# Feature attention and experts on one core: where small ties and token sums run, and when the first chunk's operands and the first weights are made

## The chip, the cores and the metric

The kernel runs on one core of a Trainium2 chip. The metric is the device time of one execution in microseconds; the kernel before was timed three times. Each engine of the core (TensorE, VectorE, ScalarE, GpSimd, and SyncE, which issues all the DMAs here) works through a queue of its own in order, and waits for the others by semaphores.

## The reference

Two parts follow each other. The first is attention with random features, for 4 batches, 8 heads, 576 tokens and 64 values a head:

```python
def phi(x):                                   # x is q or k, scaled
    proj = np.einsum('bhsd,md->bhsm', x, omega)
    h = proj - np.sum(x * x, axis=-1, keepdims=True) / 2.0
    h = h - np.max(h, axis=-1, keepdims=True)
    return np.exp(h) / np.sqrt(m)
kv = np.einsum('bhsm,bhsd->bhmd', k_p, v)
num = np.einsum('bhsm,bhmd->bhsd', q_p, kv)
den = np.einsum('bhsm,bhm->bhs', q_p, z)[..., None] + 1e-06
```

Its output, 2304 tokens of 512 values, goes into a mixture of 8 experts: a gate (`x @ w_gate`, then 8 rounds of normalizing rows and columns), and for each expert `np.maximum(x @ w1[e], 0) @ w2[e]`, weighted by the gate and summed over the experts.

## The kernel before

**Attention stage.** The work is cut into 36 jobs: 18 for k, 18 for q. A job takes half the heads of 256 rows (or the remaining 64 rows of two batches, `kr` and `qr`) through steps: transposes on TensorE (L323), a copy of them, the products with omega (`pp`, L335), the maxima on VectorE (L338, into `sqs`), the offset `cn` (L340, from the maxima and the sums of squares), the exponentials (L348 to L351), then for k the products with v (L360), for q transposes (L415), the products with kv (L435), the division (L438 to L442) and transposes (L453) into the token layout `xf`. The list `jobs` gives the order: k first, then k and q in turn, at the end q alone. In each turn of the loop one job is started and every job under way goes one step (`tick`), so the jobs overlap. `ensure_loads` issues the loads of q, k and v some jobs ahead, and calls `squares` for the keys of the jobs to come (a key serves two jobs).

**Squares.** `squares` computes the sums of squares of a key: a Square on ScalarE into a scratch `sq` (two buffers), then a fold by halves on GpSimd (L302, L303) and a negation (L304). Ahead of the Square stands a *tie*: eight numbers of the newest `cn` are written into the scratch (L297, on GpSimd), so that the Square can't be placed before that job. Two other places have such ties: the first weights' load (L177) and the first split of w1 (L221).

**Token operands.** Three chunks of 768 tokens. When a chunk's tokens are there, `token_operands` makes seven operands of it, one a tick: sums or differences of quarters of `xf` in place (L110: on GpSimd for the first two chunks, on VectorE for the last), a rounded copy (`xs`, L125, ScalarE) and the difference from it (L126, VectorE). Each operand is written to DRAM (`xd`, L128) from one of four buffers; those of the last chunk are used at once (`first`), the others are read back later. `xf` has two buffers.

**Expert stage.** 16 units of half an expert; in each, seven first-layer products a chunk (`first`, L549) and seven second-layer products a token pair (`second`, L650), with weights that `stage` loads and `split` takes apart into a rounded part and the rest (L190 on GpSimd, L222 on ScalarE, L223). The first unit's w1 is loaded and split during the attention stage, at fixed places of the job list.

The order in which each engine gets its instructions isn't that of the program: it is fixed when the program is built, by a planner that puts an instruction in as soon as its operands are there by its own reckoning, earlier program text first. The ties are there to steer it.

Of the kernel before, what the change touches and what calls it, by code (L numbers as in the profile page):

```python
# [12 lines left out]
ALU = mybir.AluOpType  # L13
AX = mybir.AxisListType


def raw(ap):

    return ap.bitcast(F32)
# [3 lines left out]
def moe_attention_kernel(  # L23
# [23 lines left out]
    nc = tc.nc  # L47
# [43 lines left out]
    ORDER = [1, 5, 6, 3, 7, 2, 4]  # L91
# [4 lines left out]
    def token_tile():  # L96
        return xs.tile([P, 2, 2, HL], F32R, tag="xs", bufs=XSB, name="xs")

    def token_operands(c, x):

        def q(r, h):
            h = 1 - h
            return x[:, 2 * r : 2 * r + 2, h * HL : (h + 1) * HL]

        last = c == NCH - 1
        gate_steps = logits(c, x)
        next(gate_steps)

        def sub(o, a, b):
            (nc.vector if last else nc.gpsimd).tensor_tensor(o, a, b, op=ALU.subtract)  # L110

        for i in ORDER:
            if i == 5:
                sub(q(0, 0), q(0, 1), q(0, 0))
            elif i == 6:
                sub(q(0, 0), q(1, 1), q(0, 0))
            elif i == 7:
                sub(q(0, 1), q(1, 1), q(0, 1))  # L120
            elif i == 4:
                sub(q(0, 0), q(1, 0), q(0, 0))
            o = {3: q(1, 1), 7: q(0, 1), 2: q(1, 0)}.get(i, q(0, 0))
            t = token_tile()
            nc.scalar.copy(t[:, 0], o)  # L125
            nc.vector.tensor_tensor(t[:, 1], o, raw(t[:, 0]), op=ALU.subtract)  # L126
            xdram[c, i] = xd.tile([P, 2, 2, HL], F32, name=f"xd{c}_{i}")
            nc.sync.dma_start(out=xdram[c, i], in_=raw(t))  # L128
            if last:
                xop[0, c, i] = t  # L130
                first(0, c, i, 0)
                first(0, c, i, 1)
            next(gate_steps, None)
            yield


    def logits(c, x):


        nt = CT // 2  # L140
        lgs = []
        for h in range(2):
            lp = bank("lp")
            for k in range(KD):
                nc.tensor.matmul(
                    lp[k * GC : (k + 1) * GC, :HL], lhsT=wgs[:, k, :], rhs=x[:, k, h * HL : (h + 1) * HL],
                    start=True, stop=True,
                )
            lg = sc.tile([P, HL], F32, tag="lg", bufs=2, name="lg")
            nc.scalar.copy(lg, lp[:, :HL])  # L150
            lgs.append(lg)
        yield
        for h, lg in enumerate(lgs):
            gp = bank("gp")
            for j in range(nt):
                nc.tensor.transpose(gp[:, j * P : (j + 1) * P], lg[:, j * P : (j + 1) * P], ident)
            t0 = c * CT + h * nt
            nc.vector.tensor_reduce(
                prob[:, t0 : t0 + nt, :],
                gp[:, : nt * P].rearrange("p (t a e) -> p t e a", a=KD, e=GC)[:, :, :E, :],  # L160
                axis=AX.X, op=ALU.add,
            )
# [4 lines left out]
    tmp = {}  # L167

    last_cn = []

    def stage(u, w):
        e, fb = units[u]
        f0 = fb * FB * P
        for r in range(2):
            wst[u, w, r] = t = wp.tile([P, 2, 2, HD], F32, tag="st", bufs=4, name="st")
            if u == 0:
                nc.gpsimd.tensor_copy(t[:, 0, 0, :8], last_cn[-1])  # L177
            if w == 1:
                src = w1[e][r * HD : (r + 1) * HD, f0 : f0 + FB * P]
            else:  # L180
                src = w2[e][f0 + r * HD : f0 + (r + 1) * HD, :]
            nc.sync.dma_start(out=t.rearrange("p k h c -> p k (h c)"), in_=src.rearrange("(k p) c -> p k c", p=P))

    def split(u, w, i):

        def q(r, h):
            return wst[u, w, r][:, :, 1 - h if w == 1 else h]

        def tt(o, a, b, op=ALU.subtract):
            nc.gpsimd.tensor_tensor(o, a, b, op=op)  # L190


        if w == 1:

            if i == 5:
                tmp[u] = wp.tile([P, 2, HD], F32, tag="t", bufs=1, name="t")
                tt(tmp[u], q(0, 1), q(1, 1), ALU.add)
            elif i == 6:
                tt(tmp[u], tmp[u], q(0, 0))
            elif i == 3:  # L200
                tt(tmp[u], q(1, 0), tmp[u])
            elif i == 7:
                tt(q(0, 1), q(0, 0), q(0, 1))
            o = {1: q(0, 0), 7: q(0, 1), 2: q(1, 0), 4: q(1, 1)}[i] if i not in (5, 6, 3) else tmp[u]
        else:

            if i == 5:
                tt(q(0, 0), q(0, 1), q(0, 0))
            elif i == 6:
                tt(q(0, 0), q(0, 0), q(1, 1))  # L210
            elif i == 7:
                tt(q(0, 1), q(1, 1), q(0, 1))
            elif i == 4:
                tt(q(0, 0), q(1, 0), q(0, 0), ALU.add)
            o = {3: q(1, 1), 7: q(0, 1), 2: q(1, 0)}.get(i, q(0, 0))
        pool = wp if w == 1 else op_
        bufs = 7 * w
        hi = pool.tile([P, 2, HD], F32R, tag=f"w{w}h", bufs=bufs, name="wh")
        lo = pool.tile([P, 2, HD], F32R, tag=f"w{w}l", bufs=bufs, name="wl")
        if u == 0 and w == 1:  # L220
            nc.gpsimd.tensor_copy(hi[:, 0, :8], last_cn[-1])  # L221
        nc.scalar.copy(hi, o)  # L222
        (nc.vector if u > 0 or (w == 2 and i in (1, 6, 7, 4)) else nc.gpsimd).tensor_tensor(lo, o, raw(hi), op=ALU.subtract)  # L223
        wt[u, w, i] = (hi, lo)
# [20 lines left out]
    def prepare_gate():  # L245

        nc.gpsimd.memset(wgs, 0.0)
        nc.sync.dma_start(out=wgs[:, :, :E], in_=w_gate.rearrange("(k p) e -> p k e", p=P))
# [37 lines left out]
    sqt = {}  # L286
# [3 lines left out]
    def squares(which, key):  # L290

        t = rawt[which, key]
        n = 1 if key[0] == "r" else 2
        s = sc.tile([P, H, n, D], F32, tag="sq", bufs=2, name="sq")
        o = sc.tile([P, H, n, 3], F32, tag="sqs", bufs=10, name="sqs")
        if last_cn:
            nc.gpsimd.tensor_copy(s.rearrange("p h j d -> p (h j d)")[:, :8], last_cn[-1])  # L297
        nc.scalar.activation(s, t[:, :H], AF.Square, scale=1.0 / math.sqrt(2.0 * math.sqrt(D)))
        w = D
        while w > 2:  # L300
            w //= 2
            nc.gpsimd.tensor_tensor(s[..., :w], s[..., :w], s[..., w : 2 * w], op=ALU.add)  # L302
        nc.gpsimd.tensor_tensor(o[..., :1], s[..., :1], s[..., 1:2], op=ALU.add)  # L303
        nc.gpsimd.tensor_scalar_mul(o[..., 2], o[..., 0], -1.0)  # L304
        sqt[which, key] = o
# [103 lines left out]
    def q_job(key, hh, t0):  # L409
# [48 lines left out]
        if done_q[c] == CT:  # L458
            yield from token_operands(c, xf[c])
# [234 lines left out]
    jobs = []  # L694

    def k_of(b):
        return [("k", (b, i // 2), i % 2) for i in range(4)]

    def q_of(b):
        return [("q", (b, i // 2), i % 2, 4 * b + i // 2 * 2) for i in range(4)]  # L700

    def kr(p):
        return ("k", ("r", p), 0)

    def qr(p):
        return ("q", ("r", p), 0, 4 * B + p)

    def mix(a, b):
        o = []
        for i in range(max(len(a), len(b))):  # L710
            o += a[i : i + 1] + b[i : i + 1]
        return o

    jobs += k_of(0) + [kr(0)]
    jobs += mix(k_of(1), q_of(0))
    jobs += mix(k_of(2) + [kr(1)], q_of(1) + [qr(0)])
    jobs += mix(k_of(3), q_of(2))
    jobs += q_of(3) + [qr(1)]

    need, seen = [], set()  # L720
# [20 lines left out]
    def tick():  # L741
        for it in list(active):
            jb, gen = it
            try:
                next(gen)
            except StopIteration:
                active.remove(it)

    ensure_loads(0)
    for i, jb in enumerate(jobs):  # L750
        if i == 12:
            prepare_gate()
        if i == 16:
            stage(0, 1)
        if i >= 22 and i % 2 == 0 and (i - 22) // 2 < 7:
            split(0, 1, ORDER[(i - 22) // 2])
        if i == 30:
            stage(0, 2)
        gen = k_job(jb[1], jb[2]) if jb[0] == "k" else q_job(*jb[1:])
        active.append((jb, gen))  # L760
        tick()
        ensure_loads(i + 1)
# [19 lines left out]
    for j, i in enumerate(ORDER):  # L782
        split(0, 2, i)
        if j < AHEAD:
            first(*todo.pop(0))

    gate = sinkhorn()
    for s, (u, n) in enumerate(steps):
        c = n // (CT // 2)
# [11 lines left out]
        for k, i in enumerate(ORDER):  # L801
# [3 lines left out]
            if k < ((5, 5, 4) if s > 2 else (3, 4, 3))[n % 3] and todo:  # L805
                pc = todo.pop(0)
                first(*pc)
                j = ORDER.index(pc[2])
# [44 lines left out]
```

## Time and profile before

| | us |
|---|---|
| median of three runs (lowest, highest) | 1634.56 (1632.02, 1638.07) |
| the profiled execution | 1634.42 |
| its span, first to last instruction | 1632.6 |
| TensorE busy in the span | 1584.5 |
| VectorE busy | 1379.9 |
| ScalarE busy | 777.3 |
| GpSimd busy | 312.4 |

A span's busy time counts instructions that compute; what an engine waits or issues is not in it. The attention stage fills about the first 200 us of the span, the experts the rest. The engines are named PE (TensorE), PEld (its weight loads), DVE (VectorE), ACT (ScalarE), POOL (GpSimd) and SP (SyncE) in the profile; L126 is line 126 of the kernel before.

### The profile page before, as it was taken

Reading aid. Unit: us, or ns where it says so; the run is one execution under the profiler, and the core shown is the slowest. Engines: PE = TensorE matmul, PEld = TensorE weight load, DVE = VectorE, ACT = ScalarE, POOL = GpSimd, SP = SyncE. Lnnn points to the kernel's source line nnn. Section 1 sums busy time; section 2 is a strip of 40 time slices with the busy share of each in tenths; the row PEclk is TensorE's granted clock in tenths of the full one; section 3 lists DMA queues with packets and bytes.
Section 4 is the critical chain, followed back from the end, with each engine's and each line's share of the span. In section 5 each row is a group of like instructions: output and inputs, shape, how many; then the busy total and the mean of one; then the engine's idle time right before and its main releaser. Section 6 shows DMA issues by size and latency. Waiting matters only on the chain.

```text
span 1632.6 us, 31484 instructions
## 1 busy us (share of the span) xinstructions
PE 1584.5 (97%) x12318; PEld 1551.6 (95%) x12318; DVE 1379.9 (85%) x2714; ACT 777.3 (48%) x1396; POOL 312.4 (19%) x340
## 2 busy tenths in 40 slices
PE   7899799999999999999999999999999999999998
PEld 5778699999999999999999999999999999999997
DVE  3788888998888898989888888989898888889777
ACT  5788654544434444534444444434344444444333
POOL 5585230111111010201111111102011111110003
PEclk9999999999999999999999999999999999999999
DMA  9442866666656565666565665656666556655562
GB/s 237 122 157 73 329 246 216 216 208 218 201 195 213 186 221 198 222 204 232 204 219 197 203 217 179 229 193 229 203 220 218 205 197 206 213 178 192 181 226 77
DMA packets 105315, 329.80 MB, mean 202 GB/s; under 512 B 14800, under 2 KB 43984, under 8 KB 105168
## 3 DMA queue, kind: packets, MB, share of 16 engines
q1 hardware_dynamic: 105168, 327.79, 59.5%
q8 instruction: 98, 1.61, 0.4%
q14 instruction: 49, 0.40, 0.1%
HBM read 306.53 MB, written 21.23 MB: 201 GB/s over the span
## 4 chain that ended last, share of the span: by engine, by line
PE 86%; DVE 7%; ACT 2%; POOL 2%; DMA 2%; issue 1%; SPq 0%; DVEq 0%; ACTq 0%; POOLq 0%
PE hx L549 24%; PE x L650 23%; PE hz L549 18%; PE z L650 11%; PE w L650 6%; PE pp L335 2%; DVE out L676 1%; DVE sm L586 1%; POOL sq L302 1%; DVE bl L586 1%; DVE sqs L338 1%; PE kv L360 1%; DVE xs L126 1%; ACT ex L348 0%; DMA xs<-xd 0%
## 5 line engine op out<-in xcount | busy, mean ns | idle before, releaser
L549 PE MATMUL hx<-xs,wh 128*128 128x384 f32 x1536 | 374.3, 337 | 2.0 <-ACT xs L125 1.4
L676 DVE SCALAR_TENSOR_TENSOR out<-x,prob,out 128x256 f32<-128x256 f32 x497 | 233.3, 476 | 65.8 <-PE x L650 64.3
L549 PE MATMUL hz<-xs,wh 128*128 128x384 f32 x1152 | 281.5, 336 | 2.1 <-ACT xs L125 1.1
L549 PEld LDWEIGHTS hx<-xs,wh 128*128 128x128 f32 x1536 | 270.1, 189 | 3.5 <-issue 3.2
L190 POOL TENSOR_TENSOR st<-st 128x512 f32<-128x512 f32 x80 | 131.7, 1646 | 700.1 <-DVE wl L223 697.1
L549 PEld LDWEIGHTS hz<-xs,wh 128*128 128x128 f32 x1152 | 202.4, 188 | 2.9 <-issue 1.3
L549 PE MATMUL hx<-xs,wl 128*128 128x384 f32 x768 | 199.4, 337 | 0.0
L628 ACT ACTIVATE bh<-hr 128x512 fp32r<-128x512 f32 x144 | 91.2, 634 | 222.0 <-PE x L650 217.0
L676 DVE SCALAR_TENSOR_TENSOR out<-z,prob,out 128x256 f32<-128x256 f32 x252 | 120.0, 476 | 58.0 <-PE z L650 57.2
L222 ACT CAST wh<-st 128x512 fp32r<-128x512 f32 x176 | 105.1, 621 | 110.9 <-PE hx L549 44.8
L624 ACT CAST sh<-sm 128x512 fp32r<-128x512 f32 x144 | 89.7, 623 | 139.9 <-PE z L650 100.1
L549 PE MATMUL hz<-xs,wl 128*128 128x384 f32 x576 | 150.1, 335 | 0.0
L549 PEld LDWEIGHTS hx<-xs,wl 128*128 128x128 f32 x768 | 138.9, 189 | 0.0
L586 DVE SCALAR_TENSOR_TENSOR sm<-hr,sm 128x256 f32<-128x256 f32 x288 | 133.5, 464 | 2.7
L223 DVE TENSOR_TENSOR wl<-st,wh 128x512 fp32r<-128x512 f32 x169 | 119.7, 719 | 11.6 <-ACT wh L222 11.1
L586 DVE SCALAR_TENSOR_TENSOR bl<-hr,bh 128x512 fp32r<-128x512 f32 x144 | 118.2, 821 | 3.1 <-ACT bh L628 1.5
L650 PE MATMUL z<-wh,sh 128*128 128x256 f32 x576 | 117.9, 281 | 2.8 <-ACT sh L607 2.7
L650 PE MATMUL x<-wl,sh 128*128 128x256 f32 x576 | 118.4, 282 | 0.0
L650 PE MATMUL x<-wh,sh 128*128 128x256 f32 x576 | 117.3, 284 | 0.7 <-DVE out L676 0.6
L598 ACT ACTIVATE ah<-hr 128x256 fp32r<-128x256 f32 x144 | 60.3, 419 | 120.6 <-PE x L650 98.9
L650 PE MATMUL z<-wh,sl 128*128 128x256 f32 x576 | 115.5, 282 | 1.6 <-DVE sl L608 1.6
L650 PE MATMUL z<-wl,sh 128*128 128x256 f32 x576 | 116.8, 281 | 0.0
(153 smaller groups left out, 3481.6 us busy)
## 6 DMA issues: line engine op xcount, KB each, us to landing
xs<-xd SPq DMA_DIRECT2D x329, 768.0 KB, 4.4
st<-in_moe_w_dram SPq DMA_DIRECT2D x64, 512.0 KB, 4.9
xd<-xs SPq DMA_DIRECT2D x21, 768.0 KB, 3.8
k<-in_k_dram SPq DMA_DIRECT2D x8, 512.0 KB, 6.5
v<-in_v_dram SPq DMA_DIRECT2D x8, 512.0 KB, 6.5
q<-in_q_dram SPq DMA_DIRECT2D x8, 512.0 KB, 6.2
out_dram<-out SPq DMA_DIRECT2D x32, 128.0 KB, 1.9
kr<-in_k_dram SPq DMA_DIRECT2D x4, 128.0 KB, 6.4
```

The costliest lines, as they stand in the source:

```text
L126: nc.vector.tensor_tensor(t[:, 1], o, raw(t[:, 0]), op=ALU.subtract)
L190: nc.gpsimd.tensor_tensor(o, a, b, op=op)
L222: nc.scalar.copy(hi, o)
L223: (nc.vector if u > 0 or (w == 2 and i in (1, 6, 7, 4)) else nc.gpsimd).tensor_tensor(lo, o, raw(hi), op=ALU.subtract)
L335: nc.tensor.matmul(pp[g][:, i * M : (i + 1) * M], lhsT=th[r, i], rhs=omt[r], start=True, stop=True)
L549: nc.tensor.matmul(pb, lhsT=a[:, k, g * P : (g + 1) * P], rhs=x[:, b, k, :], start=i in (1, 5, 2) and j == 0, stop=j == len(prods) - 1, sk ...
L586: nc.vector.scalar_tensor_tensor(o, in0=a, scalar=0.0, in1=b, op0=ALU.max, op1=op)
L598: nc.scalar.activation(ah, a11, AF.Relu)
L624: nc.scalar.copy(sh, sm)
L628: nc.scalar.activation(bh, a[:, 1:], AF.Relu)
L650: nc.tensor.matmul(pb, lhsT=ops[s][i][a][:, f], rhs=wt[u, 2, i][b][:, f], start=bool(start) and j == 0, stop=j == len(prods) - 1, skip_gro ...
L676: nc.vector.scalar_tensor_tensor(o, in0=pb, scalar=p, in1=o, op0=ALU.mult, op1=ALU.add)
```

## The change

The ties of squares and of the first weights' splits become a reduction over one element on VectorE (`tie_to_shift`) in place of a copy on GpSimd; the second key's squares, which had no tie, get one on GpSimd that reads the first key's sums. The sums and differences of all chunks (`sub`) run on VectorE. The first chunk's operands get a tie each, and an extra pause after the second, fourth and sixth (`i in (5, 3, 2)` in the order 1, 5, 6, 3, 7, 2, 4). The query job of the remaining rows, `qr(0)`, goes from place 22 of the job list to place 30. The first unit's w1 is loaded at job 8 in place of 16, and split at jobs 11, 13, ..., 23 in place of 22, 24, ..., 34.

```diff
         def sub(o, a, b):
-            (nc.vector if last else nc.gpsimd).tensor_tensor(o, a, b, op=ALU.subtract)
+            nc.vector.tensor_tensor(o, a, b, op=ALU.subtract)
...
             t = token_tile()
+            if c == 0:
+                tie_to_shift(t[:, 0, 0, :8])
             nc.scalar.copy(t[:, 0], o)
...
             next(gate_steps, None)
             yield
+            if c == 0 and i in (5, 3, 2):
+                yield
...
+    def tie_to_shift(o):
+
+        nc.vector.tensor_reduce(o, last_cn[-1].unsqueeze(2), axis=AX.X, op=ALU.max)
...
         if u == 0 and w == 1:
-            nc.gpsimd.tensor_copy(hi[:, 0, :8], last_cn[-1])
+            tie_to_shift(hi[:, 0, :8])
...
+        tie = s.rearrange("p h j d -> p (h j d)")[:, :8]
         if last_cn:
-            nc.gpsimd.tensor_copy(s.rearrange("p h j d -> p (h j d)")[:, :8], last_cn[-1])
+            tie_to_shift(tie)
+        elif len(sqt) == 1:
+            first_o = next(iter(sqt.values()))
+            nc.gpsimd.tensor_copy(tie, first_o.rearrange("p h j t -> p (h j) t")[:, :8, 0])
...
-    jobs += mix(k_of(2) + [kr(1)], q_of(1) + [qr(0)])
-    jobs += mix(k_of(3), q_of(2))
+    jobs += mix(k_of(2) + [kr(1)], q_of(1))
+    jobs += mix(k_of(3), q_of(2)) + [qr(0)]
...
-        if i == 16:
+        if i == 8:
             stage(0, 1)
-        if i >= 22 and i % 2 == 0 and (i - 22) // 2 < 7:
-            split(0, 1, ORDER[(i - 22) // 2])
+        if i in range(11, 25, 2):
+            split(0, 1, ORDER[(i - 11) // 2])
```

## Rows read from the trace of the kernel before

**Rows 1.** The page: busy time, share of the span, instructions.

```profile
PE 1584.5 (97%) x12318; PEld 1551.6 (95%) x12318; DVE 1379.9 (85%) x2714; ACT 777.3 (48%) x1396; POOL 312.4 (19%) x340
```

**Rows 2.** Busy time by stretch: us, engines, granted clock, DMA share, GB/s.

```profile
60.00:80.00 20.00, 18.29 (x324) 16.25 (x320) 15.20 (x38) 16.38 (x43) 11.78 (x25) 1.00 0.42 120
...
100.00:120.00 20.00, 18.72 (x261) 16.48 (x260) 17.93 (x33) 16.84 (x35) 19.00 (x23) 0.83 0.60 239
120.00:140.00 20.00, 18.81 (x325) 16.74 (x325) 16.95 (x41) 17.74 (x45) 13.15 (x28) 1.00 0.24 81
...
180.00:200.00 20.00, 14.82 (x83) 13.67 (x83) 17.21 (x21) 11.07 (x19) 5.65 (x4) 1.00 0.99 392
...
400.00:800.00 400.00, 398.53 (x2814) 396.71 (x2813) 349.59 (x669) 175.63 (x290) 55.26 (x36) 1.00 0.62 210
```

**Rows 3.** Timeline: a job's first transposes on TensorE (start us, us).

```profile
95.08 0.66 PE L323 MATMUL tp<-ident,qr 128*128 128x128 f32 x4
...
119.63 0.66 PE L323 MATMUL tp<-ident,q 128*128 128x128 f32 x4
...
134.05 0.66 PE L323 MATMUL tp<-ident,q 128*128 128x128 f32 x4
```

**Rows 4.** Timeline: the first job's offset and kv products (idle before, releaser).

```profile
13.51 0.18 DVE L340 TENSOR_REDUCE cn<-sqs 128x8 f32<-128x24 f32 x1 [2.54 <-POOL sqs L304]
...
15.95 2.00 PE L360 MATMUL kv<-v,ex 128*64 128x65 f32 x32 [1.46 <-ACT ex L351]
```

**Rows 5.** Waits, 0 to 60 us: total us, times, longest.

```profile
PE kv L360 <- ACT ex L351: 5.8, 3, 2.4
ACT sq L298 <- POOL sq L297: 5.5, 4, 1.6
```

**Rows 6.** Timeline: folds, a Square, the transposes behind it, the first weights.

```profile
36.22 3.34 POOL L302 TENSOR_TENSOR sq<-sq 128x512 f32<-128x512 f32 x5 [2.01 <-ACT sq L298]
...
40.37 1.06 ACT L298 ACTIVATE sq<-q 128x1024 f32<-128x1024 f32 x1 [1.65 <-POOL sq L297]
...
41.99 1.09 PE L415 MATMUL qp<-ident,ex 128*128 128x128 f32 x8 [1.12 <-ACT ex L351]
...
75.36 1.27 POOL L190 TENSOR_TENSOR t<-st 128x512 f32<-128x512 f32 x1 [5.36 <-DMA st<-in_moe_w_dram]
```

**Rows 7.** The chain that ended last, 0 to 280 us: start, us, what.

```profile
160.29 1.82 POOL xf L110
...
163.00 1.82 DVE xs L126
164.91 1.83 POOL xf L110
...
169.25 2.92 DVE xs L126 x2
...
184.66 5.20 DMA xd<-xs
...
200.98 0.79 PE z L650 x2
```

**Rows 8.** Groups by line and shape, 0 to 200 us: busy, mean ns.

```profile
L126 DVE TENSOR_TENSOR xs<-xf,xs 128x768 fp32r<-128x768 f32 x21 | 24.8, 1206 | 7.2 <-ACT xs L125 7.2
...
L110 POOL TENSOR_TENSOR xf<-xf 128x768 f32<-128x768 f32 x8 | 14.6, 1819 | 7.4 <-PE lp L145 4.5 <-DVE xs L126 1.9 <-DVE rd L438 0.9
...
L110 DVE TENSOR_TENSOR xf<-xf 128x768 f32<-128x768 f32 x4 | 3.8, 952 | 0.0
...
L373 DVE TENSOR_REDUCE kvs<-kv 128x4 f32<-128x8 f32 x8 | 1.2, 158 | 0.0
```

**Rows 9.** The chain, 92 to 135 us, by line.

```profile
by line: PE pp L335 20.8%; DVE sqs L338 16.3%; PE kv L360 9.8%; PE np L435 7.0%; DVE xs L126 5.7%; ACT xs L125 5.6%; issue 5.6%; ACT ex L348 5.0%; DVE th L328 4.4%; POOL xf L110 4.2%; PE tp L323 3.8%; POOL sq L302 3.5%; ACT sq L298 2.2%; PE
```

**Rows 10.** DMA issues, 90 to 215 us: count, KB, median us to landing.

```profile
qr<-in_q_dram SPq DMA_DIRECT2D x2, 128.0 KB, 4.4
```

**Rows 11.** Timeline, GpSimd: two token sums of the second chunk.

```profile
160.29 3.72 POOL L110 TENSOR_TENSOR xf<-xf 128x768 f32<-128x768 f32 x2 [4.04 <-PE lp L145]
```

## The prediction

> **What bounds the kernel now.** The page first: TensorE is busy for 97% of the span, VectorE for 85%, GpSimd for 19% [rows 1]. A share over the span hides that there are two stages, so the table by stretches comes next. From 400 to 800 us TensorE is busy for 398.53 of 400 us [rows 2]: the expert stage is TensorE's alone, the diff doesn't touch its lines, and I take its time as unchanged. Everything is decided in the attention stage, the first 200 us or so. There nobody is full: between 120 and 140 us TensorE has 18.81, VectorE 16.95, ScalarE 17.74 and GpSimd 13.15 of 20 us [rows 2]. A stage in which all are busy for 65 to 95% is bound by a chain that passes from engine to engine, so what counts is who makes whom wait.
>
> The transposes that open each job give the pace. From 119.63 to 134.05 us four jobs pass, 3.6 us each; from 95.08 to 119.63 us also four, but in 24.55 us [rows 3]. That is 24.55 - 14.4 = 10.1 us too many, in the stretch where the first chunk's operands are made: GpSimd shows 19.00 and VectorE 17.93 of 20 us, and the granted clock averages 0.83 [rows 2].
>
> At the start, the first cn comes at 13.51 us, after VectorE has stood for 2.54 us waiting for GpSimd's first sums of squares; it could have come at 10.97. GpSimd was late because the second key's folds lie between those of the first in its queue. TensorE's first kv product then comes at 15.95 after 1.46 us idle [rows 4].
>
> Then the ties: in the first 60 us ScalarE stood four times, 5.5 us in all, waiting for the 8-element GpSimd copy that releases its Square, and TensorE waited 5.8 us for exponentials before kv products, 1.46 of them the start just counted [rows 5]. One case whole: Square at 40.37 us after 1.65 us of waiting for the tie; the exponentials queued behind it on ScalarE come only then, and the transposes of those, at 41.99, found TensorE idle for 1.12 us [rows 6]. The tie itself is short; it stands in GpSimd's queue behind the folds of another key, 3.34 us for five of them [rows 6].
>
> Last, the chain at the end of the stage: two GpSimd token sums (1.82 and 1.83 us), VectorE differences of 1.82 and of 2.92 us for two, and 5.20 us of waiting for an operand's write to DRAM [rows 7].
>
> **The change, part by part.**
>
> *Start: -1.5 us.* The second key's Square must now wait for the first key's sums, so GpSimd finishes these first. Bounds: at most the 2.54 us by which cn was late [rows 4], at least nothing, if TensorE's next wait takes it up. I take TensorE's idle 1.46.
>
> *18 ties of squares from GpSimd to VectorE: -4.5 us.* TensorE idled for 5.8 - 1.46 = 4.3 us before kv products and 1.12 before the transposes [rows 5, 6]: 5.4 us behind waits of this kind. Bounds 0 and 5.4; I take 4.5, since a job that comes earlier meets its next wait earlier.
>
> *What the ties cost VectorE: +1.1 us.* The nearest operation is the reduction of 128x8 to 128x4, 0.158 us [rows 8]. 18 ties of squares and 7 of the split weights: 25 x 0.16 = 4.0 us. Between 92 and 135 us VectorE's maxima, differences and copies hold 16.3 + 5.7 + 4.4 = 26% of the chain [rows 9], so 1.1 us of it. Bounds 0 and 4.0. Seven more are in the next term. Behind a tie on VectorE's queue stand the maxima and cn, and with them TensorE's next job.
>
> *First chunk: -2.5 us.* VectorE gets 4 sums at 0.95 us (its price in the last chunk), 7 differences at the same price if nothing disturbs them (two inputs of the same size), and 7 ties: 3.8 + 6.7 + 1.1 = 11.6 us [rows 8]. Three extra pauses spread this over ten jobs instead of seven. A job takes 16.95/20 of 3.6 = 3.05 us of VectorE; with 1.16 more it is 4.21, 0.6 us over the pace, so ten jobs lose 6.1 if VectorE were filled to the last: 4.0 better than 10.1. Filled to the 90% that it shows from 100 to 120 us [rows 2], a job takes 4.67 and ten lose 10.7: 0.6 worse. At best the whole disturbance goes, with its low clock: 10.1. I take 2.5, towards the lossless end of the first pair, since GpSimd's four sums of 1.82 us (7.3) also leave the squares' way.
>
> *End of the stage: -3.5 us.* On the chain the two sums fall to 0.95 (-1.75), the difference of 1.82 us to 0.95 (-0.87), the two of 2.92 to 1.90 (-1.02): -3.6 [rows 7, 8]. The 5.20 us wait may shrink, as the earlier chunk's writes leave earlier; DMA engines are at 0.99 there [rows 2], so little of it. I count nothing for it, and -3.5. Bounds: 0, if VectorE's queue, which now also holds the sums, delays the last jobs' results as much as GpSimd did, and 3.6 + 5.2 = 8.8.
>
> *The remaining query job moved from place 22 to 30: 0.* The same instructions on each engine. Its second load waits for the same one buffer: it is issued right after the job's first transposes, and five jobs (18 us) lie before its use, against 4.4 us that such loads take here [rows 10]. It no longer needs the third chunk's buffer while the first chunk's operands are being made, which is what lets those be spread. If the cover fails, a job waits for a load.
>
> *First weights loaded at job 8, split at jobs 11 to 23: 0.* Seven casts on ScalarE and the sums and differences on GpSimd go from a crowded stretch into one where, from 60 to 80 us, ScalarE has 16.38 and GpSimd 11.78 of 20 us [rows 2]. The loads pass some q, k and v loads on SyncE's queue. GpSimd waited 5.36 us for these weights at 75 us [rows 6] with a tie behind it; such a wait would now hold back only folds. If that cover is gone, up to 5.4 us come back.
>
> Sum: -1.5 - 4.5 + 1.1 - 2.5 - 3.5 = -10.9. The profiled execution took 1634.42 us (span 1632.6, 1.8 around it), within 0.2 of the median 1634.56. **Forecast 1623.5 us.**
>
> **A rule weighed against the trace.** At 160.29 us GpSimd starts two sums that last to 164.01; a VectorE difference that starts at 163.00 takes 1.82 us and ends 0.8 after them, where 0.95 is the price of such an operation in the last chunk [rows 7, 8, 11]. The Trainium skill, SBUF — State Buffer, section "Who interferes with whom", says that a VectorE instruction with two SBUF inputs and a GpSimd instruction that reads SBUF exclude each other for a whole instruction. The trace agrees with that here. By that rule the moved sums, which have two such inputs, also wait for GpSimd's folds; the sum above holds without this sentence.
>
> **Rivals.**
> 1. *VectorE's two-input operations keep waiting for GpSimd's folds and splits.* For it: the 21 differences average 1.206 us, 0.25 over that price [rows 8], and GpSimd, mostly with folds, is busy for 11.78 to 13.15 of 20 us where no sums run [rows 2]. Against: the long GpSimd sums, beside which the 1.82 occurred, are gone. If the 21 differences and the 8 moved sums each lose 0.25 us, that is 7.3 us, more than the first chunk's and the end's gains (6.0): -10.9 + 7.3 = -3.6: **1631**.
> 2. *The ties block VectorE.* A tie writes the scratch that GpSimd folds, and there are two of them; if GpSimd is two keys behind, VectorE stands in front of the maxima until a fold ends. For it: the folds take 3.34 us and follow each other closely after 36 us [rows 6]. Against: before, the tie waited for the latest fold, now for the one before it. It decides from some 0.6 us a tie: 18 x 0.6 = 10.8 eats the gain. At 1.1 us it is 20, so -10.9 + 20 = +9: **1643.5**.
> 3. *More goes than I count:* all of the first chunk's 10.1 us (7.6 more) and half the wait for writes (2.6): **1613**.
>
> **How the numbers follow.** Chances: forecast 0.46 (its own range 1617 to 1627), rival 1 0.28, rival 2 0.10, rival 3 0.16. Under 0.5% (8.2 us) nothing can be told from no change here. Faster takes the forecast, rival 3 and nothing of rival 1: 0.62, less 0.02 for the forecast's end above 1626.4, so 0.60; the same 0.30; slower 0.10. The range runs from 1611, below rival 3, to 1635, above rival 1, and leaves out rival 2 and the end of rival 3.
>
> **What would show it.** First cn near 11 us; no wait of ScalarE for a tie on GpSimd; four jobs in about 22 us, not 24.55, around the first chunk's operands; differences near 0.95 us; the second layer's first z product some 9 to 11 us before the 200.98 us of now [rows 7]; GpSimd's busy time down by at least the eight sums' 14.6 us, VectorE's up by some 8 (8 x 0.95 + 32 x 0.16 = 12.7, less the 21 x 0.25 = 5 that the differences lose now) [rows 8]. Wrong, if VectorE shows waits for GpSimd's folds before ties, or if the expert stage takes another time than now.

## The result and the profile after

The changed kernel takes 1644.19 us (median of 4 runs, 1641.23 to 1645.85), the kernel before 1633.56 on the same chip: a ratio of 1.0059, with a 95% interval of [1.0033, 1.0084]. It is slower by 10.6 us, where 10.9 us less were forecast, and it lies outside the range of 1611 to 1635.

The page's busy times moved as the edits say. GpSimd lost 22.4 us and VectorE gained 10.8, TensorE is within 0.7 us of before [rows 1]:

```profile
PE 1583.8 (96%) x12318; PEld 1549.8 (94%) x12318; DVE 1390.7 (85%) x2754; ACT 776.5 (47%) x1396; POOL 290.0 (18%) x308
```

So the 10.6 us are not work that was added but time in which engines stood still. The table by stretches shows where (columns as in [rows 2]: busy time of TensorE, its weight loads, VectorE, ScalarE and GpSimd, then granted clock, DMA share, GB/s):

```profile
40.00:60.00 20.00, 9.92 (x132) 8.26 (x132) 7.17 (x18) 8.74 (x19) 9.46 (x17) 0.75 0.72 157
...
120.00:140.00 20.00, 14.32 (x239) 12.56 (x235) 16.90 (x36) 15.02 (x34) 12.10 (x23) 1.00 0.43 148
140.00:160.00 20.00, 15.24 (x197) 12.97 (x194) 14.05 (x39) 11.06 (x31) 4.91 (x9) 0.91 0.52 171
...
400.00:800.00 400.00, 395.45 (x2787) 392.87 (x2786) 352.70 (x664) 173.89 (x289) 54.41 (x37) 1.00 0.59 207
```

Between 40 and 60 us TensorE, VectorE and ScalarE are busy for 7 to 10 of 20 us: a stall of all of them, not an engine that is full. From 120 to 160 us TensorE is short too. From 400 to 800 us TensorE is about as full as before [rows 2]. The same view in steps of 4 us takes the first stall apart:

```profile
40.00:44.00 4.00, 3.85 (x85) 3.36 (x84) 2.06 (x5) 3.87 (x9) 0.00 (x0) 1.00 1.24 218
44.00:48.00 4.00, 1.02 (x8) 0.78 (x8) 0.00 (x0) 0.00 (x0) 0.00 (x0) 1.00 1.11 305
48.00:52.00 4.00, 0.00 (x0) 0.00 (x0) 0.00 (x0) 0.00 (x0) 2.35 (x3) 0.77 1.14 239
52.00:56.00 4.00, 1.08 (x4) 0.71 (x4) 2.99 (x9) 2.12 (x3) 3.60 (x8) 0.50 0.08 21
56.00:60.00 4.00, 3.96 (x36) 3.40 (x38) 2.12 (x5) 2.76 (x7) 3.52 (x8) 0.50 0.00 0
60.00:64.00 4.00, 4.00 (x81) 3.81 (x78) 3.17 (x10) 2.12 (x7) 2.09 (x5) 0.95 0.47 135
```

GpSimd does nothing from 40 to 48 us, the others nothing from 48 to 52, while the DMA engines are full (1.11 to 1.24); when these fall to 0.08, the work goes on. After TensorE has stood, its granted clock is 0.50, the lower level of 1.2 GHz, from 52 to 60 us; from 60 to 64 us, with TensorE busy again, it averages 0.95, so it is back at 2.4 GHz for most of that stretch.

The timeline from 34 to 62 us shows the stall from its beginning (start, duration, engine, line, operation; in brackets the idle time before it and who ended it):

```profile
39.80 2.65 SPq L190 DMA_DIRECT2D st<-in_moe_w_dram  x2
43.93 0.66 PE L335 MATMUL tp<-ident,q 128*128 128x128 f32 x4
49.65 1.26 POOL L198 TENSOR_TENSOR t<-st 128x512 f32<-128x512 f32 x1 [11.29 <-DMA st<-in_moe_w_dram]
50.87 0.32 POOL L314 TENSOR_TENSOR sq<-sq 128x64 f32<-128x64 f32 x1
52.94 0.16 DVE L177 TENSOR_REDUCE sq<-cn 128x8 f32<-128x8 f32 x1 [10.85 <-POOL sqs L315]
53.13 1.06 ACT L310 ACTIVATE sq<-q 128x1024 f32<-128x1024 f32 x1 [9.27 <-DVE sq L177]
54.01 1.08 PE L427 MATMUL qp<-ident,ex 128*128 128x128 f32 x4 [8.99 <-DVE xt L454]
58.05 1.12 PE L335 MATMUL tp<-ident,k 128*128 128x128 f32 x4
```

Read it from the top. The first weights' loads are issued from 39.80 us. The first sum of the split (L198) stands in GpSimd's queue in the middle of a fold: the fold's steps at L314 follow it. GpSimd waits 11.29 us for the load. The rest of the fold comes only then. VectorE's next tie (L177) overwrites a scratch that this fold still reads, and there are two of them, so VectorE waits 10.85 us; ScalarE's Square waits for the tie, and TensorE for what lies behind. The transposes of two jobs in a row are 58.05 - 43.93 = 14.1 us apart. In the timeline of the kernel before, the same two openings are 3.2 us apart, so 10.9 us are lost here:

```profile
49.97 0.66 PE L323 MATMUL tp<-ident,q 128*128 128x128 f32 x4
53.17 0.66 PE L323 MATMUL tp<-ident,k 128*128 128x128 f32 x4
```

A second stall lies between 134 and 152 us:

```profile
134.94 3.69 SPq L190 DMA_DIRECT2D st<-in_moe_w_dram  x4
137.99 0.66 PE L335 MATMUL tp<-ident,qr 128*128 128x128 f32 x4
139.14 1.97 SPq L280 DMA_DIRECT2D qr<-in_q_dram  x2
142.23 0.66 PE L335 MATMUL tp<-ident,q 128*128 128x128 f32 x4
147.78 0.63 ACT L310 ACTIVATE sq<-qr 128x512 f32<-128x512 f32 x1 [4.95 <-DMA qr<-in_q_dram]
148.93 1.93 PE L347 MATMUL pp<-omt,th 64*128 64x128 f32 x14 [3.57 <-ACT qt L429]
150.79 1.11 PE L335 MATMUL tp<-ident,q 128*128 128x128 f32 x4
```

The second query load of the remaining rows goes out after the first one's transposes, behind four loads of weights, and its Square stands early in ScalarE's queue: ScalarE waits 4.95 us with the copies for TensorE (qt) behind it. The chain that ended last holds both loads; at the end of the stage a sum and a difference take 0.92 and 0.96 us on it, where 1.82 stood [rows 7] (start, duration, what):

```profile
41.90 7.62 DMA st<-in_moe_w_dram
...
139.82 7.85 DMA qr<-in_q_dram
...
170.97 0.96 DVE xs L128
172.00 0.92 DVE xf L110
...
187.29 0.98 PE hx L561 x4
```

In the groups up to 210 us the operations that changed are as cheap as expected (busy us, mean ns, idle before) [rows 8]:

```profile
L128 DVE TENSOR_TENSOR xs<-xf,xs 128x768 fp32r<-128x768 f32 x21 | 20.8, 1001 | 8.0 <-ACT xs L127 8.0
L110 DVE TENSOR_TENSOR xf<-xf 128x768 f32<-128x768 f32 x12 | 11.6, 964 | 0.1
L177 DVE TENSOR_REDUCE sq<-cn 128x8 f32<-128x8 f32 x18 | 2.7, 151 | 10.8 <-POOL sqs L315 10.8
```

Before one of the 18 ties of squares VectorE stands for GpSimd, for 10.8 us; before the other seventeen it doesn't stand.

### The profile page after: what moved, and what is told of

It is laid out like the page before. It is cut to its first block, busy times and chain, and to the rows that moved or that the text cites. A ratio compares the mean times of both kernels' runs of the same rounds, so it can differ in the third digit from the quotient of the medians.

```text
span 1641.4 us, 31461 instructions
## 1 busy us (share of the span) xinstructions
PE 1583.8 (96%) x12318; PEld 1549.8 (94%) x12318; DVE 1390.7 (85%) x2754; ACT 776.5 (47%) x1396; POOL 290.0 (18%) x308
## 4 chain that ended last, share of the span: by engine, by line
PE 86%; DVE 9%; ACT 2%; DMA 1%; issue 1%; POOL 1%; SPq 0%; ACTq 0%; DVEq 0%; POOLq 0%
PE hx L561 24%; PE x L662 23%; PE hz L561 18%; PE z L662 11%; PE w L662 6%; PE pp L347 2%; DVE sm L598 1%; DVE out L688 1%; DVE sqs L350 1%; DVE wl L231 1%; DVE bl L598 1%; PE np L447 1%; PE tp L335 1%; DVE sl L637 1%; PE kv L372 1%
## 5 line engine op out<-in xcount | busy, mean ns | idle before, releaser
L198 POOL TENSOR_TENSOR st<-st 128x512 f32<-128x512 f32 x80 | 127.9, 1599 | 726.3 <-DVE wl L231 721.1
L598 DVE SCALAR_TENSOR_TENSOR sm<-hr,sm 128x256 f32<-128x256 f32 x288 | 138.8, 482 | 2.6
L231 DVE TENSOR_TENSOR wl<-st,wh 128x512 fp32r<-128x512 f32 x169 | 123.8, 743 | 9.8 <-ACT wh L230 9.5
L662 PE MATMUL x<-wh,sl 128*128 128x256 f32 x576 | 117.1, 282 | 0.5 <-DVE sl L637 0.5
```

Of the source, the lines that this page charges most:

```text
L598: nc.vector.scalar_tensor_tensor(o, in0=a, scalar=0.0, in1=b, op0=ALU.max, op1=op)
L662: nc.tensor.matmul(pb, lhsT=ops[s][i][a][:, f], rhs=wt[u, 2, i][b][:, f], start=bool(start) and j == 0, stop=j == len(prods) - 1, skip_gro ...
```

## The experiments

The theory: two waits for DMA loads cost the time, that of the split's first sum on GpSimd (from the early weights) and that of the second `qr` load on ScalarE (from the moved job); the rest of the change is worth about what was forecast. The rival is the prediction's second: ties on VectorE block it whenever GpSimd is behind. Every kernel here ran in three rounds beside the kernel before; medians of that one were 1633.57, 1634.17 and 1634.35 us in the three groups. All of them compute the whole reference.

**Taking one wait out of the changed kernel.** The weights back to their old jobs (weights_late); the second load into a buffer of its own kind, free long before (qr_in_kr); the weights early, but the split's sum in question tied to a later shift, so that it is queued behind the fold (sum_tied); and the last two together (sum_tied_qr).

```diff
 # e1_weights_late
-        if i == 8:
+        if i == 16:
...
-        if i in range(11, 25, 2):
-            split(0, 1, ORDER[(i - 11) // 2])
+        if i >= 22 and i % 2 == 0 and (i - 22) // 2 < 7:
+            split(0, 1, ORDER[(i - 22) // 2])
 # e2_qr_in_kr
-                t = rw.tile([P, H, 1, D], F32, tag=f"{which}r", bufs=1, name=f"{which}r")
+                t = rw.tile([P, H, 1, D], F32, tag="kr" if pr == 1 else f"{which}r", bufs=1, name=f"{which}r")
 # e4_sum_tied, in split, for the tile i == 5
+                if u == 0:
+                    tie_to_shift(tmp[u][:, 0, :8])
```

> The changed kernel with only its first-weights part undone (load at job 16, splits at jobs 22 to 34). Theory A, two single waits: the changed kernel loses some 11 us where GpSimd waits 11.3 us for the first weights with a fold behind it and VectorE's tie waits 10.8 us for that fold, and some 8 us where ScalarE waits for the second load of the remaining query rows. Undoing the early weights takes the first wait away and puts the splits back beside the first chunk's operands: 1644 - 11 + 1 to 2 = about 1634 to 1636, job 11 no longer 14 us after job 10. Theory B, VectorE has become too full (some 40 more instructions and the sums), and the waits only show its slack: 1641 to 1644.

> The changed kernel, with the second load of the remaining query rows going into the buffer of the remaining key rows, which is free long before, so that it need not wait for the first one's transposes. Theory A: the 4.9 us wait of ScalarE and what hangs on it go, about 8 us: 1636. Theory B: 1642 to 1644. Rival within A: if the lateness of that load was only the queue of writes ahead of it, half of it stays, 1640.

> The changed kernel, weights still early, but the first sum of the first weights gets a tie on VectorE of its own, so that the planner cannot place it on GpSimd ahead of job 13's part of the program. Theory A: the 11.3 us wait of GpSimd goes, without moving any load or split: 1644 - 11 = 1633. Theory B: 1643. If the early load itself did the harm (its DMA traffic among the q, k and v loads), nothing changes either: 1643.

> Both mends in one: the tied sum and the second load of the remaining query rows in the key rows' buffer. Theory A: both waits go, 1644 - 11 - 8 = 1625, about 9 us under the kernel before. Theory B: 1641 or more.

| kernel | us | ratio to before |
|---|---|---|
| weights_late | 1628.19 | 0.9958 [0.9943, 0.9973] |
| qr_in_kr | 1639.75 | 1.0033 [1.0022, 1.0044] |
| sum_tied | 1631.01 | 0.9983 [0.9973, 0.9992] |
| sum_tied_qr | 1627.18 | 0.9952 [0.9937, 0.9967] |

weights_late came out 6 to 8 us faster than expected, sum_tied 2 faster, sum_tied_qr 2 slower, and qr_in_kr 4 slower than the 1636 of the theory, at the 1640 of the rival within it: the first wait costs more than the theory had it, the second only about half. With only the sum tied, 13.2 us come back, with only the buffer 4.4; both together give 17.0, so they add up within 0.6. The timeline of sum_tied has the load at nearly the same time, and the two openings 3.1 us apart:

```profile
39.49 2.56 SPq L190 DMA_DIRECT2D st<-in_moe_w_dram  x2
42.93 0.66 PE L337 MATMUL tp<-ident,q 128*128 128x128 f32 x4
46.06 0.66 PE L337 MATMUL tp<-ident,k 128*128 128x128 f32 x4
```

The DMA engines are as full as in the changed kernel (1.05 to 1.26 in steps of 4 us from 40 to 56 us), and TensorE is busy for 15.14 of these 16 us. So neither the early load's traffic nor the splits' work makes this stall; the place of one sum in GpSimd's queue does. The `qr` buffer is worth 4.4 us beside the changed kernel and 3.8 beside sum_tied. In qr_in_kr that load is issued at 97.29 us, and ScalarE's Square at 144.96 follows the operation before it without a pause. GpSimd stands in that kernel too, 9.29 us up to 148.79, in front of a load for a sum of the next unit's weights (9.69 us in the changed kernel), and yet TensorE is busy for 10.80 of the 12 us from 140 to 152: a wait of nearly the same length as the first, at a place where no other engine soon needs what stands behind it.

**Parts alone, added to the kernel before, and the rival put to the test.** The ties of squares with the second key's tie (ties_alone); all token sums on VectorE (sums_alone); sum_tied with the query job back at place 22 and without the first chunk's pauses (no_move); and the changed kernel with its square ties back on GpSimd (ties_on_pool).

```diff
 # f1_ties_alone, against before
+    def tie_to_shift(o):
...
+        tie = s.rearrange("p h j d -> p (h j d)")[:, :8]
         if last_cn:
-            nc.gpsimd.tensor_copy(s.rearrange("p h j d -> p (h j d)")[:, :8], last_cn[-1])
+            tie_to_shift(tie)
+        elif len(sqt) == 1:
+            first_o = next(iter(sqt.values()))
+            nc.gpsimd.tensor_copy(tie, first_o.rearrange("p h j t -> p (h j) t")[:, :8, 0])
 # f2_sums_alone, against before
-            (nc.vector if last else nc.gpsimd).tensor_tensor(o, a, b, op=ALU.subtract)
+            nc.vector.tensor_tensor(o, a, b, op=ALU.subtract)
 # f3_no_move, against sum_tied
-            if c == 0 and i in (5, 3, 2):
-                yield
...
-    jobs += mix(k_of(2) + [kr(1)], q_of(1))
-    jobs += mix(k_of(3), q_of(2)) + [qr(0)]
+    jobs += mix(k_of(2) + [kr(1)], q_of(1) + [qr(0)])
+    jobs += mix(k_of(3), q_of(2))
 # f5_ties_on_pool, against the changed kernel
-            tie_to_shift(tie)
+            nc.gpsimd.tensor_copy(tie, last_cn[-1])
```

> The kernel before with one part of the change alone: the 18 ties of squares on VectorE and the tie of the second key's squares. The prediction's terms for it: start -1.5, ties -4.5, their cost on VectorE 18/25 of 1.1 = +0.8, so -5.2: 1628.4. If ties on VectorE are harmful in themselves (the prediction's rival in which they block it): 1636 or more. If the waits only move: 1634.

> The kernel before with one part alone: the token sums of the first two chunks on VectorE. The prediction's terms: end of the stage -3.5, and of the first chunk's -2.5 the part without the spreading, 0 to -2: 1628 to 1630. Rival, VectorE is the bound there and takes back what GpSimd gave: 1634 to 1637.

> The changed kernel with the first weights' sum tied, as in e4, and with the job of the remaining query rows back at place 22 and the first chunk's three extra pauses taken out. It has neither wait for a load. If the move and the pauses are worth something beyond the wait that they bring, it comes out above the 1627.2 of the kernel with both waits mended, by the prediction's 2.5 us or so: 1629 to 1631. If they are worth nothing, 1627 or less.

> The changed kernel with the ties of squares back on GpSimd, everything else as changed. GpSimd still waits for the early weights with a fold behind it. If it was VectorE standing in front of its tie that turned this wait into a stall of all engines, most of the 11 us go and the waits of ScalarE for ties come back: 1636 to 1639. If GpSimd's wait stalls the stage in any case, since the ties and ScalarE's Squares stand behind it too, nothing is won and the ties' gain is lost: 1645 to 1650.

| kernel | us | ratio to before |
|---|---|---|
| ties_alone | 1626.79 | 0.9952 [0.9937, 0.9967] |
| sums_alone | 1632.12 | 0.9986 [0.9977, 0.9996] |
| no_move | 1626.25 | 0.9949 [0.9934, 0.9965] |
| ties_on_pool | 1653.49 | 1.0114 [1.0091, 1.0136] |

The rival falls with ties_on_pool. If VectorE's ties were the cause, this kernel should have been faster than the changed one; it is 9.3 us slower, above even the 1645 to 1650 that were expected if GpSimd's wait stalls the stage in any case. The same stall stands in its timeline, one job earlier and now on ScalarE directly:

```profile
44.02 0.66 PE L335 MATMUL tp<-ident,k 128*128 128x128 f32 x4
49.15 1.26 POOL L198 TENSOR_TENSOR t<-st 128x512 f32<-128x512 f32 x1 [4.72 <-DMA st<-in_moe_w_dram]
52.51 1.06 ACT L310 ACTIVATE sq<-k 128x1024 f32<-128x1024 f32 x1 [8.28 <-POOL sq L306]
59.00 1.08 PE L335 MATMUL tp<-ident,q 128*128 128x128 f32 x4
```

GpSimd stands in front of the load, and whoever needs GpSimd next stands too. The ties alone are worth 7.4 us (the rival had 1636 or more), which is above their terms of 1.5 + 4.5 less VectorE's price, 5.2; the sums alone 2.1, less than the 4 to 6 of their terms but not the loss of the rival. no_move came out as expected if move and pauses are worth nothing.

**The other two parts alone, the two good parts together, and both loads mended the other way.** Early weights (weights_alone); the moved job with the first chunk's pauses and ties (move_alone); ties, split ties and sums on VectorE, with the order, the pauses and the weights as before (ties_sums); and the changed kernel with late weights and the `qr` buffer (late_qr).

```diff
 # g1_weights_alone, against before: e1's edit the other way round
-        if i == 16:
+        if i == 8:
 # g2_ties_sums, against before: f1's and f2's edits, and
-            nc.gpsimd.tensor_copy(hi[:, 0, :8], last_cn[-1])
+            tie_to_shift(hi[:, 0, :8])
 # g3_move_alone, against before: f3's edit the other way round, and
+            if c == 0:
+                tie_to_shift(t[:, 0, 0, :8])
 # g4_late_qr, against the changed kernel: e1's and e2's edits
```

> The kernel before with one part alone: the first weights loaded at job 8 and split at jobs 11 to 23. If the early weights are the cause by themselves, GpSimd waits some 8 to 11 us for them near 40 to 50 us and the stage stands still: 1642 to 1648. If they harm only together with ties on VectorE or the moved job: 1634.

> The kernel before with the parts that won on their own: ties of squares and of the splits on VectorE, the second key's tie, all token sums on VectorE; job order, pauses and weights as before. If the gains add, 1634.2 - 7.4 - 2.1 = 1624.7, and it is the fastest so far. If the sums' gain was only that GpSimd was late, which the ties have already mended: 1626.8.

> The kernel before with one part alone: the job of the remaining query rows at place 30, the first chunk's pauses and ties. If this part brings the wait for the second load of these rows (some 4.4 us won back when it was taken away) and nothing else: 1637 to 1639. If spreading the operands pays as much: 1634. By the prediction's terms (first chunk's -2.5, move 0): 1632.

> The changed kernel with both waits taken away by the other mend of the weights: loaded and split as before, and the second load of the remaining query rows in the key rows' buffer. From 1628.2 with late weights alone, less the part of the second wait that is still there: 1624 to 1627. Against the kernel with ties and sums alone it tells whether move and pauses are worth anything: equal, nothing; slower, they cost.

| kernel | us | ratio to before |
|---|---|---|
| weights_alone | 1644.69 | 1.0072 [1.0051, 1.0093] |
| ties_sums | 1624.71 | 0.9942 [0.9925, 0.9958] |
| move_alone | 1641.84 | 1.0048 [1.0033, 1.0063] |
| late_qr | 1628.99 | 0.9967 [0.9957, 0.9977] |

Early weights alone cost 10.3 us, in a kernel whose ties are all on GpSimd. Its timeline has the same waits behind the same sum, and the two openings around them 16.65 us apart, where 5.86 passed before:

```profile
42.78 0.66 PE L323 MATMUL tp<-ident,k 128*128 128x128 f32 x4
49.58 1.26 POOL L190 TENSOR_TENSOR t<-st 128x512 f32<-128x512 f32 x1 [6.40 <-DMA st<-in_moe_w_dram]
52.94 1.06 ACT L298 ACTIVATE sq<-k 128x1024 f32<-128x1024 f32 x1 [9.96 <-POOL sq L297]
59.43 0.90 PE L323 MATMUL tp<-ident,q 128*128 128x128 f32 x4
```

ties_sums is the fastest of all kernels here, 9.6 us below the kernel before; ties_alone and sums_alone add up to 7.4 + 2.1 = 9.5, as expected if the gains add. By the table of stretches, its TensorE has nearly twice the busy time of the changed kernel's from 40 to 60 us, at a granted clock of 1.00:

```profile
40.00:60.00 20.00, 19.19 (x332) 16.93 (x328) 16.96 (x45) 18.18 (x44) 11.27 (x26) 1.00 0.88 184
```

By its chain from 140 to 185 us the first expert product (hx) starts at 163.57 us, where it starts at 187.29 in the changed kernel. The chain of the kernel before is the second row:

```profile
163.57 0.97 PE hx L557 x4
```

```profile
175.73 2.60 PE hx L549 x12
```

Not all of such a lead is kept: from there to the end of the span pass 1459.0 us in ties_sums, 1456.9 before and 1454.1 in the changed kernel.

late_qr missed its 1624 to 1627. It is 4.3 us slower than ties_sums, from which it differs by the moved job, the first chunk's pauses and ties, and the buffer; its expectation read "slower" as move and pauses costing time. And the buffer brought nothing over weights_late, 1628.99 against 1628.19. The timeline of weights_late says why: two loads of weights are issued ahead, not four, and ScalarE waits 0.37 us for its load, not 4.95:

```profile
124.87 0.90 SPq L190 DMA_DIRECT2D st<-in_moe_w_dram  x2
...
131.76 0.63 ACT L310 ACTIVATE sq<-qr 128x512 f32<-128x512 f32 x1 [0.37 <-DMA qr<-in_q_dram]
```

The DMA issues from 100 to 155 us, first of weights_late and then of the changed kernel, give the same load's time from issue to landing, against 4.4 us before [rows 10]:

```profile
qr<-in_q_dram SPq DMA_DIRECT2D x2, 128.0 KB, 3.9
```

```profile
qr<-in_q_dram SPq DMA_DIRECT2D x2, 128.0 KB, 8.0
```

The second wait is thus in part a consequence of the early weights: the same job at the same place waits 4.95 us with them, 4.21 with them when the sum is tied, and 0.37 without. That the weights ahead of it delay the load is read from these rows and was not tried alone.

Move_alone, at +7.5 us, went past its expectations and isn't explained by the load: there ScalarE waits 1.42 us for it. The last five distances between job openings take 160.81 - 137.49 = 23.3 us there, against 153.95 - 134.05 = 19.9 before. That is 3.4 of the 7.5; another 2.1 lie in the first chunk's stretch (eight jobs in 41.1 us, against 39.0). The timelines of TensorE show that the last five distances are longer in every kernel with the move and the pauses: they take 22.65 to 28.35 us in all eight of them, and 19.9 in all six that have neither. no_move has the first chunk's ties and still 19.9, so the ties don't cause it; whether the move or the pauses do is open, since every kernel has both or neither. Part of it seems to come back later where the sums are on VectorE: from the first expert product to the end of the span late_qr takes 1454.3 us, ties_sums 1459.0, and move_alone, with the sums on GpSimd, 1458.5. What is left is 4.3 us between late_qr and ties_sums, about 1 between sum_tied_qr and no_move, whose weights are early, and 7.5 in move_alone. Why it differs so much stays open.

## Why the prediction was wrong

**The failed steps** are the two terms set at 0 with a cover named. With both waits taken out (sum_tied_qr) the change is worth -6.4 us in place of +10.6; the other 4.5 us to the -10.9 of the forecast are terms that were mis-sized, further below.

*"First weights loaded at job 8, split at jobs 11 to 23: 0."* Measured alone +10.3 us, and 13.2 us come back when one sum is tied later. The step argued from the busy times of 60 to 80 us, that there is room, and said that a wait for the weights "would now hold back only folds". Both failed. The wait falls between 40 and 50 us, where the DMA engines are full and the load takes 7.62 us in the chain; and folds are not "only" folds: two scratches tie VectorE's and ScalarE's queues to them, so 11.29 us on GpSimd arrive almost whole at TensorE as 10.9. The bound of 5.4 us was taken from the wait at 75 us [rows 6], where the DMA share is 0.42 [rows 2], not 1.11 to 1.24. For another place in the order it was no bound.

*"The remaining query job moved from place 22 to 30: 0."* The cover was to be five jobs, 18 us, before the second load's use. The order of ScalarE's queue decides the use, not the job's place: ScalarE came to the Square 4.8 us after the first one's transposes began (147.78 - 4.95 - 137.99), while the load, issued 1.2 us after they began, took 8.0, not 4.4 [rows 10]. Taking the wait out is worth 4.4 us. Nor does the move, with the pauses that it was to allow, pay for itself: no_move, with neither, is about 1 us faster than sum_tied_qr, ties_sums 4.3 us faster than late_qr.

**Rival 2** gave 1643.5 and described VectorE standing before a tie until a fold ends. Its time is near the measured one by luck, for its cause is not the one found: before seventeen of eighteen ties VectorE doesn't stand, GpSimd isn't two keys behind from folding, it is stopped by a load, and with the ties on GpSimd the stall is still there, with openings 59.00 - 44.02 = 15.0 us apart, where the same two stood 5.9 apart before. The prediction's own sign of being wrong, a wait of VectorE for a fold ahead of a tie, did show, but once and behind that load.

**What held.** The first cn comes at 11.14 us in place of 13.51 [rows 4], as foretold (10.97 was the limit):

```profile
10.86 0.19 POOL L309 COPY sq<-sqs 128x8 f32<-128x8 f32 x1
11.14 0.18 DVE L352 TENSOR_REDUCE cn<-sqs 128x8 f32<-128x24 f32 x1
```

The four ScalarE waits for ties on GpSimd [rows 5] are gone; the second key's new tie brings one of 3.51 us at the start, where it is meant. And the job that opened at 49.97 us opens at 43.93, 6.0 us earlier: start and ties were set at 6.0. Their whole worth, with what they cost VectorE, was 7.4 where 5.2 was forecast. A tie costs 0.151 us, where 0.16 was taken. The differences take 1.001 us in place of 1.206, 0.05 above the price forecast, so rival 1 fell too: the differences lose 0.05 us each and the sums 0.01 (964 ns against 952), not 0.25, though GpSimd still folds beside them. The Trainium skill, SBUF — State Buffer, section "Who interferes with whom", says that a VectorE instruction with two SBUF inputs contends with a GpSimd instruction that reads SBUF, for a shared pair of ports that is an exclusive lock. That the differences got faster as GpSimd's sums went, to 0.976 in sums_alone, agrees with it, in this group up to 195 us of that kernel:

```profile
L126 DVE TENSOR_TENSOR xs<-xf,xs 128x768 fp32r<-128x768 f32 x21 | 20.2, 976 | 4.6 <-ACT xs L125 4.4
```

**What was mis-sized.** The end of the stage, at -3.5, measured -1.7: from the last job's transposes to the first expert product 175.73 - 153.95 = 21.78 us pass before, 20.04 in sums_alone; all of the moved sums together were worth 2.1. The first chunk, at -2.5: eight jobs there take 39.0 us before, 38.1 in sums_alone and 36.7 in ties_sums, so about what was forecast comes, but without the pauses and the move; in sum_tied_qr, which has them, it is 39.7. Each sum and tie was well priced by itself; what the end of the stage waits for in their place was not followed up. That ties and sums without the two moves give -9.6, near the -10.9, is in part luck: the ties brought 2.2 more than their terms, the sums less. The expert stage was taken as unchanged; from its first product on it is 2.8 us shorter in the changed kernel.

## What to carry to other kernels

On engines that work in order, the cost of an operation that waits for a load isn't its duration but its place: look at what stands behind it in its queue, and follow that to the engine that sets the pace. An edit priced at nothing needs its cover worked out where the operation will then stand: when its load is issued there, what else is in the DMA queues, and when its user comes up in the queue, not in the list of jobs. The version to keep is ties_sums: small ties and all sums on VectorE, and the loads where they were.

## What the runs showed of the hardware

A load's time from issue to landing hung on its company more than expected: the same pair of 128 KB loads took 3.9 us behind two loads of weights and 8.0 behind four; that the loads ahead are the reason was not tried alone. And the stall of some 9 us left a second cost behind: from 52 to 60 us, in which TensorE took up its work again, it ran at the lower level of its clock, and sixteen products with omega took 2.08 us at 56.04 us, where sixteen of them had taken 1.16 before the stall:

```profile
42.84 1.16 PE L347 MATMUL pp<-omt,th 64*128 64x128 f32 x16
56.04 2.08 PE L347 MATMUL pp<-omt,th 64*128 64x128 f32 x16 [0.95 <-DVE th L340]
```

In sum_tied, without the stall, the granted clock is 1.00 from 40 to 56 us. How much of the 10.9 us is the clock's was not measured apart. An estimate from these rows: TensorE's 1.08 + 3.96 = 5.0 us of work in that stretch would have taken 5.0 x 1.16 / 2.08 = 2.8 us at the upper level, so 2.2 us at most.
